# A thinner background share, a second buffer for raw columns, and a first pair turned in smaller pieces

## The chip, the cores and the metric

The kernel runs on one core of one Trainium2 chip. The metric is the device time of one execution in microseconds (us); 1149.14 us is the median of three runs of the kernel before (1148.28 to 1150.97). Beside them stands one execution that the hardware profiler recorded.

## The reference, cut to what matters

```python
def _attn_ref(q, k, v):                      # (4, 8, 576, 64) each
    q_rot, k_rot = (rotate(q), rotate(k))    # rotary embedding, two halves of 32
    scores = scale * np.matmul(q_rot, k_rot.transpose(0, 1, 3, 2))
    scores = scores - np.max(scores, axis=-1, keepdims=True)
    attn = np.exp(scores)
    attn = attn / (np.sum(attn, axis=-1, keepdims=True) + 1e-09)
    return np.matmul(attn, v)

def reference(**kwargs):
    x = attention output as (2304, 512)
    x = g1(x @ w_in) @ w_out                 # 512 -> 2048 -> 512
    return g2(x @ w_in2) @ w_out2            # 512 -> 2048 -> 512
```

g1 is a piecewise square, g2 is s times the square of the positive part, plus b. Everything is float32.

## The kernel before, in words

**Arithmetic.** Most operands of TensorE are split into a high part, rounded to the fast float32 format that TensorE takes, and the rest as a low part; a product is then made of three matmuls (high by high, high by low, low by high). ScalarE writes the high parts, VectorE or GpSimd the low parts. The weights arrive as 64-bit floats and are converted by a chain of two ScalarE, four VectorE and four GpSimd instructions for every 512 columns (`Slice.convert`, lines 115 to 134).

**Attention.** The 32 (batch, head) pairs are taken two heads at a time: 16 pairs of heads, four for each batch. Every pair is cut into 9 units, so there are 144 units. A unit is 128 rows of scores of one head against all 576 keys (unit 4 of a pair takes the last 64 rows of both heads): `qk` (line 325) runs the score matmuls (L339) into one of two PSUM tiles `sc`, VectorE takes the negated row maximum (L341), ScalarE the exponential (L346, which frees `sc`), then `tmain` transposes the result on TensorE (L361), and after units 4 and 8 of a pair `finish` multiplies by v (L387 to L394) and scales.

Before its scores a pair is turned by its rotary angles. `rope_pair` (line 273) multiplies by the table `tab_sb` (L279) and adds (L281); `lay_q` (line 287) writes each head's q as a high part in that head's own 64 partitions (ScalarE, L294) and the low part in the other 64 (VectorE, L295); `lay_k` (line 297) writes k's high part `kh` into both partition halves and its low part `kz` into one. For the first pair `lay_k` copies the high part on ScalarE (L315), has the second copy made by a DMA that SP issues (L316), and has GpSimd write the low part (L317). The first pair is turned in two pieces of 288 columns, all of it ahead of unit 0 (lines 468 to 475). Pair i+1 is turned during pair i: q at the pair's unit 0, k at unit 2 (`do_load`, line 515).

**Background work ("items").** When the four pairs of a batch are done, the first layer can begin on that batch's columns. `beside` (line 441) is a generator: it first loads raw columns `xs` from memory and splits them into `xh` and `xl` (`split_x`, line 432; four loads for each chunk of 288 columns, one `xs` buffer), lets 4 turns pass (LEAD), and then yields once after each item of 12 matmuls at line 171 (4 items `h` with their activation, then 4 items `y` with their store, for each chunk and group of weights). Three such jobs of 20, 52 and 20 turns (LEAD among them) are appended at steps 41, 75 and 111, 92 turns in all. `do_fill` (line 566) runs once in each of the steps n = 48 to 147 and hands `run_fill` a share of a turn: 0.85 below step 90 and 0.98 from there. What is left after the last step runs at once (`while fill: run_fill(1.0)`, line 579). A share left over when no job is waiting is forgotten (line 504).

**Order.** One program order is given; a scheduler that simulates the engines decides at build time in which order each engine gets its instructions (for TensorE until line 687, from where its order is as written). `issue_after(x)` puts the instructions of a block behind x, but only those on x's own engine. `first`, the last instruction that laying the first pair's k returns, is a DMA on SP; so the later loads on SP stand behind it (lines 476 and 575).

**After attention.** Five stages (lines 691 to 695) run the remaining columns of the first layer and the whole second one, matmul behind matmul.

Of the kernel before, what the change touches and what calls it, by code (L numbers as in the profile page):

```python
# [8 lines left out]
F32 = mybir.dt.float32  # L9
# [4 lines left out]
AF = mybir.ActivationFunctionType  # L14
ALU = mybir.AluOpType
AX = mybir.AxisListType
# [3 lines left out]
B, H, S, D = 4, 8, 576, 64  # L20
# [3 lines left out]
P = 128  # L24
# [35 lines left out]
N1 = 288  # L60
# [3 lines left out]
def kernel(ctx, tc, qq, kk, vv, tab, ww1, ww2, s, b, out):  # L64
    nc = tc.nc
# [14 lines left out]
    def pool_tt(out, in0, in1, op, dim=-1):  # L80

        n = out.shape[dim]
        free = 1
        for x in out.shape[1:]:
            free *= x
        k = min(n, -(-free // PW))
        for i in range(k):
            c = [slice(None)] * len(out.shape)
            c[dim] = slice(n * i // k, n * (i + 1) // k)
            c = tuple(c)  # L90
            nc.gpsimd.tensor_tensor(out=out[c], in0=in0[c], in1=in1[c], op=op)  # L91
# [3 lines left out]
    def split(dst_hi, dst_lo, src, hi_eng, lo_eng):  # L95
        if hi_eng is nc.scalar:
            made.append(nc.scalar.copy(dst_hi, src).ins)  # L97
        else:
            hi_eng.tensor_copy(dst_hi, src)
        tt = pool_tt if lo_eng is nc.gpsimd else nc.vector.tensor_tensor  # L100
        tt(out=dst_lo, in0=src, in1=dst_hi, op=ALU.subtract)  # L101
# [2 lines left out]
    HW = 512  # L104


    exps, tps = {}, {}

    class Slice:

# [113 lines left out]
    m2 = p1.enter_context(tc.tile_pool(name="m2", bufs=2, reuse_waits="tile"))  # L224
# [10 lines left out]
    tab_sb = att.tile([P, 2, S], F32, name="tab_sb")  # L235
# [4 lines left out]
    qk_in, v_in, stacks = {}, {}, {}  # L240

    WHOLE = [slice(0, S)]
    HALVES = [slice(0, 288), slice(288, S)]

    def load_qk(i, nm, pieces=WHOLE):
        bb, hp = divmod(i, NP)
        t = att2.tile([P, 2, S], F32, tag="qkin", name=f"{nm}in", bufs=QB)
        for c in pieces:
            nc.sync.dma_start(out=t[:, :, c], in_=(qq if nm == "q" else kk)[bb, hp, :, :, c])
        qk_in[nm, i] = t  # L250
# [22 lines left out]
    def rope_pair(i, nm, mul, add, lo_eng, pieces=WHOLE):  # L273

        t = qk_in.pop((nm, i))
        tt = {nc.gpsimd: pool_tt, nc.vector: nc.vector.tensor_tensor}
        last = None
        for c in pieces:
            tt[mul](out=t[:, :, c], in0=t[:, :, c], in1=tab_sb[:, :, c], op=ALU.mult)  # L279
            r = t[:, 1, c]  # L280
            tt[add](out=r, in0=t[:, 0, c], in1=r, op=ALU.add)  # L281
            last = (lay_q if nm == "q" else lay_k)(i, t, c, lo_eng)
        return last

    SELF = [slice(0, D), slice(D, P)]

    def lay_q(i, t, c, lo_eng):

        st = stacks["q", i] = qs_t[i % 2]
        r = t[:, 1, c]  # L290
        for j in range(2):
            own, other = SELF[j], SELF[1 - j]
            at = slice(j * QW + c.start, j * QW + c.stop)
            nc.scalar.activation(st[own, at], r[own], AF.Copy, scale=0.125)  # L294
            nc.vector.scalar_tensor_tensor(out=st[other, at], in0=r[own], scalar=0.125, in1=st[own, at], op0=ALU.mult, op1=ALU.subtract)  # L295

    def lay_k(i, t, c, lo_engs):
        if c.start == 0:
            stacks["k", i] = att.tile([P, 2, S], F32R, tag="kh", name="kh", bufs=2), kz_t[i % 2]
        kh, kz = stacks["k", i]  # L300
        tt = {nc.gpsimd: pool_tt, nc.vector: nc.vector.tensor_tensor}
        r = t[:, 1, c]
        if i > 0:
            hi, lo = t[:, 0, c].bitcast(F32R), r.bitcast(F32R)
            nc.scalar.copy(hi, r)
            pool_tt(out=lo, in0=r, in1=t[:, 0, c], op=ALU.subtract)
            for j in range(2):
                own = SELF[j]
                for rows in SELF:
                    nc.sync.dma_start(out=kh[rows, j, c].bitcast(F32), in_=t[own, 0, c])  # L310
                m = nc.sync.dma_start(out=kz[own, j, c].bitcast(F32), in_=t[own, 1, c])
            return m.ins
        for j in range(2):
            own, other = SELF[j], SELF[1 - j]
            nc.scalar.copy(kh[own, j, c], r[own])  # L315
            m = nc.sync.dma_start(out=kh[other, j, c].bitcast(F32), in_=kh[own, j, c].bitcast(F32))  # L316
            tt[lo_engs[j]](out=kz[own, j, c], in0=r[own], in1=kh[own, j, c], op=ALU.subtract)  # L317
        return m.ins

# [5 lines left out]
    def qk(i, k):  # L325
        if k == 0:
            sums_t[i] = att2.tile([P, 9], F32, tag="sums", name="sums")
        j, t = UNITS[k]
        sc = ps_s.tile([P, 2, 512], F32, tag="sc", name="sc")
        if j is None:  # L330
            places = [(0, 512), (1, S + D)]
        else:
            places = [(j, t * P + j * (QW + D))]
        straight = [[(0, 0, 288)], [(0, 288, 288)]]
        moved = [[(0, D, 288)], [(0, 352, 224), (224, 0, D)]]
        for half in range(2):
            todo = [(stacks["q", i][:, c:c + P], r[:, h], w) for h, c in places for r in stacks["k", i] for w in (moved if j is None and h == 0 else straight)[half]]
            for m, (l, r, (o, k0, n)) in enumerate(todo):
                nc.tensor.matmul(sc[:, half, o:o + n], l, r[:, k0:k0 + n], start=m == 0, stop=m == len(todo) - 1)  # L339
        nm = att.tile([P, 1], F32, tag="nm", name="nm", bufs=4)  # L340
        nc.vector.tensor_reduce(out=nm, in_=sc[:, :, :288], axis=AX.XY, op=ALU.max, negate=True)  # L341
        if j != 1:
            p_t[i, t] = att.tile([P, 2 * S], F32, tag="p", name="p", bufs=PB)
        p = p_t[i, t][:, S * (j == 0):S * (j == 0) + S]
        col = 4 if j is None else 2 * t + j + t // 2
        exps[i * 9 + k] = nc.scalar.activation(p, sc[:, :, :288], AF.Exp, bias=nm, scale=1.0, accum_out=sums_t[i][:, col:col + 1]).ins  # L346
        if j is None:
            nc.scalar.copy(p_t[i, t][:, S:S + D], p[:, 512:])
# [83 lines left out]
    def split_x(c):  # L432
        xh = m1.tile([P, KD, N1], F32R, tag="xh", name="xh")
        xl = m1.tile([P, KD, N1], F32R, tag="xl", name="xl")
        for k in range(KD):
            xs = m2.tile([P, N1], F32, tag="xs", name="xs", bufs=1)
            nc.sync.dma_start(out=xs, in_=xd[k, :, c * N1:(c + 1) * N1])
            split(xh[:, k, :], xl[:, k, :], xs, nc.scalar, nc.gpsimd)
        return xh, xl
# [31 lines left out]
        if c is HALVES[0]:  # L471
            load_qk(0, "k", HALVES)
    load_qk(0, "q", HALVES)
    first = rope_pair(0, "k", nc.vector, nc.vector, [nc.gpsimd, nc.gpsimd], HALVES)
    rope_pair(0, "q", nc.vector, nc.vector, None, HALVES)
    with tc.issue_after(first):
        load_qk(1, "k")
        load_qk(1, "q")
# [17 lines left out]
    def run_fill(budget):  # L496
        nonlocal done
        done += budget
        while fill and done > 0:
            try:  # L500
                done -= next(fill[0])
            except StopIteration:
                fill.pop(0)
        if not fill:
            done = 0.0
# [7 lines left out]
            qk(i, k)  # L513

    def do_load(n):
        if n < len(units):
            i, k = units[n]
            if i + 1 < NPAIR:
                if k == 0:
                    rope_pair(i + 1, "q", nc.gpsimd if i else nc.vector, nc.vector, None)  # L520
                elif k == 2:
                    rope_pair(i + 1, "k", nc.gpsimd, nc.gpsimd, [nc.gpsimd, nc.vector])
                elif k == 3:
                    load_v(i + 1)
                elif k in (4, 6) and i + 2 < NPAIR:
                    load_qk(i + 2, "q" if k == 4 else "k")

        if n in range(33, 51, 2) or n in range(70, 110, 4):
            with tc.issue_after(exps[n - 14]):
                convert()  # L530

        if n in PARK_AT and parking:
            with tc.issue_after(exps[n - 4]):
                parking.pop(0).park(wst, scratch)
# [31 lines left out]
    def do_fill(n):  # L566
        if n < 48:
            return
        with tc.issue_after(exps[min(n, len(units)) - 4]):
            run_fill(0.85 if n < 90 else 0.98)  # L570

    acts = {"q": do_qk, "l": do_load, "t": do_t, "a": do_av, "f": do_fill}
    for n in range(len(units) + LA):
# [106 lines left out]
    def cut(n0, n1, n):  # L680

        k = -(-(n1 - n0) // n)
        at = [n0 + (n1 - n0) // 16 * i // k * 16 for i in range(k + 1)]
        return [(a, b - a) for a, b in zip(at, at[1:])]
# [5 lines left out]
    a, b, c, d = cut(last, NT, N2A), cut(0, last, N2), cut(last, NT, N2), cut(0, NT, N2)  # L690
# [57 lines left out]
```

## Time and profile before

| | us |
|---|---|
| median of three runs | 1149.14 |
| the profiled execution, its own time | 1153.25 |
| the profiled execution, its span (first to last instruction) | 1151.5 |
| TensorE (PE) busy in the span | 1098.2 |
| ScalarE (ACT) busy | 696.0 |
| VectorE (DVE) busy | 603.2 |
| GpSimd (POOL) busy | 533.0 |

PE is the matmul engine; PEld is the loading of its stationary operand, which overlaps. SP is the engine that issues the DMAs. L339 is line 339 of the kernel. "Idle before" is the time that an engine stood still ahead of an instruction, and the arrow names what ended it. Matmuls are pipelined and their ends are modelled, so a busy PE is not PE at its peak. Durations below come from the one profiled execution; it took 4.1 us more than the median of the runs.

### The profile page before, as it was taken

How to read it: one execution, taken by the hardware profiler on the slowest of the kernel's cores; microseconds unless marked ns; L12 is line 12 of the kernel's file. 1: busy time of each engine (PE TensorE's matmuls, PEld its weight loads, DVE VectorE, ACT ScalarE, POOL GpSimd, SP SyncE). 2: the span in 40 equal slices, each digit the busy share in tenths (PEclk: the TensorE clock that was granted, in tenths of full speed). 3: DMA queues.
4: the chain of work that ended last, by engine and by line, in shares of the span. 5: the costliest groups of instructions: out<-in, count | busy, mean ns of one | idle time of the engine just before them, and what ended most of it. 6: DMA issues, size and time to landing. Idle time of an engine off the chain costs nothing.

```text
span 1151.5 us, 18669 instructions
## 1 busy us (share of the span) xinstructions
PE 1098.2 (95%) x6720; PEld 984.0 (85%) x6720; DVE 603.2 (52%) x999; ACT 696.0 (60%) x1466; POOL 533.0 (46%) x716
## 2 busy tenths in 40 slices
PE   4898889899989999999999999999999999999998
PEld 3566688688888988999999999999888889888887
DVE  6788878877666574455565645434333342221221
ACT  4676767766667765565554544377666666555443
POOL 6888878875544230355655634424432452111000
PEclk9999899999999999999999999999999999999999
DMA  7665645554554441544544533313322322321210
GB/s 218 170 198 141 176 143 172 181 158 123 150 170 131 145 140 45 179 144 153 150 137 147 146 121 109 88 58 102 96 80 86 115 91 68 99 66 43 67 50 34
DMA packets 90076, 140.75 MB, mean 122 GB/s; under 512 B 28928, under 2 KB 67072, under 8 KB 89984
## 3 DMA queue, kind: packets, MB, share of 16 engines
q1 hardware_dynamic: 89984, 139.56, 40.0%
q8 instruction: 53, 0.87, 0.3%
q14 instruction: 39, 0.32, 0.1%
HBM read 95.22 MB, written 30.74 MB: 109 GB/s over the span
## 4 chain that ended last, share of the span: by engine, by line
PE 75%; POOL 5%; DVE 5%; DMA 4%; ACT 3%; issue 3%; SPq 1%; POOLq 0%; ACTq 0%
PE hps L171 29%; PE yps L662 10%; PE yps L663 10%; PE yps L661 10%; PE sc L339 4%; DMA xs<-xd 3%; PE av L387 3%; PE h L171 3%; PE y L171 3%; PE tp L361 2%; POOL kin L91 2%; ACT p L346 1%; DVE nm L341 1%; POOL xl L91 1%; POOL wm L91 1%
## 5 line engine op out<-in xcount | busy, mean ns | idle before, releaser
L171 PE MATMUL hps<-xh,w 128*128 128x464 f32 (+5 forms) x1216 | 344.0, 348 | 0.0
L171 PEld LDWEIGHTS hps<-xh,w 128*128 128x128 f32 x1216 | 221.7, 188 | 14.8
L661 PE MATMUL yps<-gh,w 128*128 128x464 f32 (+5 forms) x608 | 211.7, 348 | 0.0
L662 PE MATMUL yps<-gl,w 128*128 128x464 f32 (+5 forms) x608 | 211.5, 348 | 0.1
L663 PE MATMUL yps<-gh,w 128*128 128x464 f32 (+5 forms) x608 | 211.6, 348 | 0.0
L171 PE MATMUL hps<-xl,w 128*128 128x464 f32 (+5 forms) x608 | 211.5, 348 | 0.0
L91 POOL TENSOR_TENSOR xl<-xs,xh 128x232 fp32r<-128x232 f32 (+5 forms) x172 | 125.4, 754 | 177.5 <-ACT xh L97 177.0
L101 DVE TENSOR_TENSOR gl<-ar,gh 128x464 fp32r<-128x464 f32 (+1 forms) x80 | 59.4, 743 | 264.7 <-ACT gh L97 264.7
L91 POOL TENSOR_TENSOR wm<-wm,w 128x256 f32<-128x256 f32 x112 | 98.7, 901 | 204.0 <-ACT w L132 180.8
L339 PE MATMUL sc<-kh,qs 128*128 128x288 f32 x336 | 104.3, 331 | 40.5 <-ACT p L346 26.1
L341 DVE TENSOR_REDUCE nm<-sc 128x1 f32<-128x576 f32 x144 | 107.1, 751 | 51.1 <-PE sc L339 50.1
L346 ACT ACTIVATE p<-sc,nm 128x576 f32<-128x576 f32 x144 | 106.7, 744 | 27.0 <-DVE nm L341 25.2
L662 PEld LDWEIGHTS yps<-gl,w 128*128 128x128 f32 x608 | 114.1, 188 | 7.8 <-DVE gl L101 0.3
L663 PEld LDWEIGHTS yps<-gh,w 128*128 128x128 f32 x608 | 114.1, 188 | 7.4
L661 PEld LDWEIGHTS yps<-gh,w 128*128 128x128 f32 x608 | 114.1, 188 | 7.4
L171 PEld LDWEIGHTS hps<-xl,w 128*128 128x128 f32 x608 | 114.1, 188 | 7.3
L202 ACT ACTIVATE ar<-hps 128x464 f32<-128x464 f32 (+1 forms) x80 | 44.4, 555 | 123.0 <-PE hps L171 122.4
L339 PEld LDWEIGHTS sc<-kh,qs 128*128 128x128 f32 x336 | 64.9, 196 | 60.9 <-ACT p L346 35.3
L101 DVE TENSOR_TENSOR gl<-ac,gh 128x288 fp32r<-128x288 f32 (+3 forms) x112 | 75.6, 675 | 39.2 <-ACT gh L97 38.5
L339 PE MATMUL sc<-kz,qs 128*128 128x288 f32 x336 | 95.3, 303 | 0.6 <-DMA kz<-kin 0.6
L361 PE MATMUL tp<-ident,p 128*128 128x128 f32 x576 | 90.1, 280 | 0.5 <-DVE ac L194 0.5
L91 POOL TENSOR_TENSOR w<-wm,wa 128x256 fp32r<-128x256 f32 x112 | 87.5, 798 | 1.4 <-DVE wa L131 1.4
(84 smaller groups left out, 1988.6 us busy)
## 6 DMA issues: line engine op xcount, KB each, us to landing
wraw<-in_ww SPq DMA_DIRECT2D x64, 512.0 KB, 3.9
kin<-in_k SPq DMA_DIRECT2D x15, 576.0 KB, 4.1
qin<-in_q SPq DMA_DIRECT2D x15, 576.0 KB, 4.3
kh<-kin SPq DMA_DIRECT2D x60, 144.0 KB, 2.6
xs<-y1d SPq DMA_DIRECT2D x32, 232.0 KB, 2.5
xs<-xd SPq DMA_DIRECT2D x44, 144.0 KB, 2.5
yd<-ys SPq DMA_DIRECT2D x40, 144.0 KB, 2.5
xd<-u SPq DMA_DIRECT2D x16, 288.0 KB, 2.4
```

Of the source, the lines that this page charges most:

```text
L91: nc.gpsimd.tensor_tensor(out=out[c], in0=in0[c], in1=in1[c], op=op)
L101: tt(out=dst_lo, in0=src, in1=dst_hi, op=ALU.subtract)
L171: m = nc.tensor.matmul(out_ps, l, r, start=(i == 0), stop=(i == n - 1))
L202: nc.scalar.activation(r, h, AF.Relu)
L339: nc.tensor.matmul(sc[:, half, o:o + n], l, r[:, k0:k0 + n], start=m == 0, stop=m == len(todo) - 1)
L341: nc.vector.tensor_reduce(out=nm, in_=sc[:, :, :288], axis=AX.XY, op=ALU.max, negate=True)
L346: exps[i * 9 + k] = nc.scalar.activation(p, sc[:, :, :288], AF.Exp, bias=nm, scale=1.0, accum_out=sums_t[i][:, col:col + 1]).ins
L361: m = nc.tensor.transpose(v[:, c, :], p[:, c * P:(c + 1) * P], ident)
L387: nc.tensor.matmul(ps[j * D:(j + 1) * D, :n], v[:, kt, j, :], pt[g][:, kt, j, :], start=kt == 0, stop=False)
L661: nc.tensor.matmul(acc, wh, gh, start=f == 0, stop=False)
L662: nc.tensor.matmul(acc, wh, gl, start=False, stop=False)
L663: nc.tensor.matmul(acc, wl, gh, start=False, stop=last)
```

## The change

- `run_fill` is handed 0.62 of a turn below step 76 and 0.92 from there (before: 0.85 below step 90, 0.98 from there).
- `xs`, the tile of raw columns in `split_x`, gets two buffers in place of one.
- For the first pair, the second copy of k's high part is written by ScalarE from the turned k; the DMA at L316 goes. `first` is then a ScalarE instruction, and so `issue_after(first)` holds back ScalarE's instructions, no longer SP's.
- The first pair's q is turned in three pieces (columns 0 to 127, 128 to 287, 288 to 575) in place of two. Ahead of unit 0 stand k and the first piece alone, with head 0 before head 1; the second piece follows in step 0, the third in step 1, behind the maximum of unit 0 on VectorE.
- The second pair's q is turned at unit 1 in place of unit 0, its VectorE instructions behind the maximum of unit 1; the ScalarE instructions of its k stand behind the exponential of unit 2.

```diff
-    def lay_q(i, t, c, lo_eng):
+    def lay_q(i, t, c, lo_eng, heads=range(2)):
...
-        for j in range(2):
+        for j in heads:
...
-            nc.scalar.activation(st[own, at], r[own], AF.Copy, scale=0.125)
-            nc.vector.scalar_tensor_tensor(out=st[other, at], in0=r[own], scalar=0.125, in1=st[own, at], op0=ALU.mult, op1=ALU.subtract)
+            h = nc.scalar.activation(st[own, at], r[own], AF.Copy, scale=0.125)
+            m = nc.vector.scalar_tensor_tensor(out=st[other, at], in0=r[own], scalar=0.125, in1=st[own, at], op0=ALU.mult, op1=ALU.subtract)
+        return h.ins, m.ins
...
             nc.scalar.copy(kh[own, j, c], r[own])
-            m = nc.sync.dma_start(out=kh[other, j, c].bitcast(F32), in_=kh[own, j, c].bitcast(F32))
+            m = nc.scalar.copy(kh[other, j, c], r[own])
...
-            xs = m2.tile([P, N1], F32, tag="xs", name="xs", bufs=1)
+            xs = m2.tile([P, N1], F32, tag="xs", name="xs", bufs=2)
...
-    first = rope_pair(0, "k", nc.vector, nc.vector, [nc.gpsimd, nc.gpsimd], HALVES)
-    rope_pair(0, "q", nc.vector, nc.vector, None, HALVES)
+    QP = [slice(0, P), slice(P, 288), slice(288, S)]
+    turned_by(tk, HALVES[0])
+    lay_k(0, tk, HALVES[0], [nc.gpsimd, nc.gpsimd])
+    turned_by(tk, HALVES[1])
+    lay_k(0, tk, HALVES[1], [nc.gpsimd, nc.gpsimd], [0])
+    turned_by(tq, QP[0])
+    hi, rest = lay_q(0, tq, QP[0], None, [0])
+    with tc.issue_after(hi):
+        first = lay_k(0, tk, HALVES[1], [nc.gpsimd, nc.gpsimd], [1])
+    hi, rest = lay_q(0, tq, QP[0], None, [1])
...
     def do_load(n):
+        if n < 2:
+            with tc.issue_after(maxs[0] if n else rest):
+                turned_by(tq, QP[n + 1])
+                lay_q(0, tq, QP[n + 1], None)
...
-                if k == 0:
-                    rope_pair(i + 1, "q", nc.gpsimd if i else nc.vector, nc.vector, None)
+                if k == (i == 0):
+                    with ExitStack() if i else tc.issue_after(maxs[1]):
+                        rope_pair(i + 1, "q", nc.gpsimd if i else nc.vector, nc.vector, None)
                 elif k == 2:
-                    rope_pair(i + 1, "k", nc.gpsimd, nc.gpsimd, [nc.gpsimd, nc.vector])
+                    with ExitStack() if i else tc.issue_after(exps[2]):
+                        rope_pair(i + 1, "k", nc.gpsimd, nc.gpsimd, [nc.gpsimd, nc.vector])
...
-            run_fill(0.85 if n < 90 else 0.98)
+            run_fill(0.62 if n < 76 else 0.92)
```

`turned_by` is the multiplication by the table and the addition of lines 279 and 281, on VectorE; `maxs[n]` is unit n's maximum (L341) and `exps[n]` its exponential (L346).

## Rows read from the trace of the kernel before

**Rows 1.** Busy time by stretch: us, then PE, PEld, DVE, ACT, POOL, clock, DMA, GB/s.

```profile
13.30:127.20 113.90, 101.56 (x682) 72.52 (x682) 97.47 (x152) 78.09 (x179) 92.77 (x123) 0.97 0.66 190
127.20:204.80 77.60, 69.17 (x505) 60.49 (x502) 62.93 (x103) 53.23 (x130) 61.38 (x79) 0.96 0.50 147
204.80:227.00 22.20, 18.32 (x130) 13.71 (x130) 19.23 (x32) 14.63 (x36) 19.88 (x26) 0.92 0.69 217
227.00:345.30 118.30, 110.12 (x833) 97.20 (x831) 83.27 (x142) 77.85 (x194) 69.87 (x93) 0.99 0.51 148
345.30:451.10 105.80, 102.31 (x798) 90.85 (x799) 64.89 (x123) 71.12 (x179) 31.63 (x49) 1.00 0.42 125
...
480.00:1140.00 660.00, 660.00 (x3532) 616.53 (x3532) 256.55 (x416) 381.30 (x704) 243.82 (x324) 1.00 0.32 99
```

**Rows 2.** Instructions in order of time, the first 14 us: start, us, engine, line.

```profile
6.73 5.04 SPq L316 DMA_DIRECT2D kh<-kh  x4
...
8.25 0.80 DVE L279 TENSOR_TENSOR kin<-kin,tab_sb 128x576 f32<-128x576 f32 x1 [2.01 <-DMA tab_sb<-in_tab]
9.05 0.76 DVE L279 TENSOR_TENSOR qin<-qin,tab_sb 128x576 f32<-128x576 f32 x1
9.72 0.45 DVE L281 TENSOR_TENSOR kin<-kin 128x288 f32<-128x288 f32 x1
...
10.21 0.88 ACT L315 CAST kh<-kin 64x288 fp32r<-64x288 f32 x2 [3.05 <-DVE kin L281]
...
12.81 1.91 DVE L295 SCALAR_TENSOR_TENSOR qs<-qin,qs 64x288 fp32r<-64x288 f32 x4
...
13.32 0.61 PE L339 MATMUL sc<-kh,qs 128*128 128x288 f32 x1 [13.32 <-DVE qs L295]
```

**Rows 3.** ACT's instructions of line 346 (two a unit) in those stretches.

```profile
13.30:127.20 113.90, 39.35 (x96) 0.97 0.66 190
127.20:204.80 77.60, 18.47 (x45) 0.96 0.50 147
...
227.00:345.30 118.30, 26.94 (x66) 0.99 0.51 148
345.30:451.10 105.80, 25.86 (x64) 1.00 0.42 125
```

**Rows 4.** PE's and PEld's instructions of line 171 (12 an item) in those stretches.

```profile
127.20:204.80 77.60, 31.83 (x192) 27.19 (x192) 0.96 0.50 147
...
227.00:345.30 118.30, 57.29 (x354) 49.54 (x354) 0.99 0.51 148
345.30:451.10 105.80, 51.56 (x330) 45.17 (x330) 1.00 0.42 125
```

**Rows 5.** What ACT waited for, 127 to 460 us: total us, times, longest.

```profile
ACT xh L97 <- DMA xs<-xd: 22.4, 18, 3.7
ACT p L346 <- DVE nm L341: 12.3, 13, 2.3
ACT ys L464 <- PE y L171: 9.5, 7, 2.7
ACT gh L97 <- DVE ac L194: 8.5, 10, 2.2
```

**Rows 6.** What PE waited for, 127 to 460 us: total us, times, longest.

```profile
PE sc L339 <- ACT p L346: 15.5, 14, 2.0
PE y L171 <- DVE gl L101: 3.0, 3, 1.4
PE h L171 <- ACT xh L97: 2.5, 1, 2.5
```

**Rows 7.** Instructions in order of time around 323 us.

```profile
323.37 0.43 ACT L97 CAST xh<-xs 128x288 fp32r<-128x288 f32 x1 [3.73 <-DMA xs<-xd]
...
323.85 0.40 PE L171 MATMUL h<-xh,w 128*128 128x288 f32 x1 [2.54 <-ACT xh L97]
```

**Rows 8.** The chain that ended last, one item among attention's end: start, us.

```profile
453.30 1.59 PE h L171 x12
```

More of the change, by code (lines that the diff above doesn't have):

```diff
@@ L104 @@
     HW = 512
-    exps, tps = {}, {}
+    exps, tps, maxs = {}, {}, {}
     class Slice:
@@ L285, with lay_k @@
     SELF = [slice(0, D), slice(D, P)]
-    def lay_q(i, t, c, lo_eng):
+    def lay_q(i, t, c, lo_eng, heads=range(2)):
         st = stacks["q", i] = qs_t[i % 2]
         r = t[:, 1, c]
-        for j in range(2):
+        for j in heads:
             own, other = SELF[j], SELF[1 - j]
             at = slice(j * QW + c.start, j * QW + c.stop)
-            nc.scalar.activation(st[own, at], r[own], AF.Copy, scale=0.125)
-            nc.vector.scalar_tensor_tensor(out=st[other, at], in0=r[own], scalar=0.125, in1=st[own, at], op0=ALU.mult, op1=ALU.subtract)
-    def lay_k(i, t, c, lo_engs):
-        if c.start == 0:
+            h = nc.scalar.activation(st[own, at], r[own], AF.Copy, scale=0.125)
+            m = nc.vector.scalar_tensor_tensor(out=st[other, at], in0=r[own], scalar=0.125, in1=st[own, at], op0=ALU.mult, op1=ALU.subtract)
+        return h.ins, m.ins
+    def lay_k(i, t, c, lo_engs, heads=range(2)):
+        if c.start == 0 and 0 in heads:
             stacks["k", i] = att.tile([P, 2, S], F32R, tag="kh", name="kh", bufs=2), kz_t[i % 2]
@@ L312, in lay_k @@
             return m.ins
-        for j in range(2):
+        for j in heads:
             own, other = SELF[j], SELF[1 - j]
             nc.scalar.copy(kh[own, j, c], r[own])
-            m = nc.sync.dma_start(out=kh[other, j, c].bitcast(F32), in_=kh[own, j, c].bitcast(F32))
+            m = nc.scalar.copy(kh[other, j, c], r[own])
             tt[lo_engs[j]](out=kz[own, j, c], in0=r[own], in1=kh[own, j, c], op=ALU.subtract)
@@ L340, in qk @@
         nm = att.tile([P, 1], F32, tag="nm", name="nm", bufs=4)
-        nc.vector.tensor_reduce(out=nm, in_=sc[:, :, :288], axis=AX.XY, op=ALU.max, negate=True)
+        maxs[i * 9 + k] = nc.vector.tensor_reduce(out=nm, in_=sc[:, :, :288], axis=AX.XY, op=ALU.max, negate=True).ins
         if j != 1:
@@ L473, with turned_by @@
     load_qk(0, "q", HALVES)
-    first = rope_pair(0, "k", nc.vector, nc.vector, [nc.gpsimd, nc.gpsimd], HALVES)
-    rope_pair(0, "q", nc.vector, nc.vector, None, HALVES)
+    tq, tk = qk_in.pop(("q", 0)), qk_in.pop(("k", 0))
+    def turned_by(t, c):
+        nc.vector.tensor_tensor(out=t[:, :, c], in0=t[:, :, c], in1=tab_sb[:, :, c], op=ALU.mult)
+        nc.vector.tensor_tensor(out=t[:, 1, c], in0=t[:, 0, c], in1=t[:, 1, c], op=ALU.add)
+    QP = [slice(0, P), slice(P, 288), slice(288, S)]
[8 more added lines that the diff above has]
+    hi, rest = lay_q(0, tq, QP[0], None, [1])
     with tc.issue_after(first):
```

## The prediction

> **What bounds the kernel now.** I read the busy time by stretch first, because a mean over the whole span hides that there are three regimes. From 480 us to 1140 us PE is busy for 660 of 660 us [rows 1]: there a change can gain nothing that isn't fewer matmuls, and this one removes none. Up to 13.3 us PE does nothing at all. Between lies attention, in which PE is short of busy by 12.3 us up to 127.2, by 8.4 us to 204.8, by 3.9 us to 227.0, by 8.2 us to 345.3 and by 3.5 us to 451.1 [rows 1], 36.3 us together. So whatever can be won stands in the 13.3 us of start and these 36.3 us; all the rest is PE's own work in whatever order.
>
> Next I asked what ends PE's idle time in the stretch with items: 15.5 us end with the exponential, which frees the score tile, and 2.5 us with `xh` [rows 6], so 18.0 us end at ACT. ACT is not full there (53.2 of 77.6 us, 77.9 of 118.3 us [rows 1]); it takes its instructions in order and stands in front of something that is late. The longest such thing is the load of the raw columns: 22.4 us in 18 waits [rows 5]. One of them shows the whole mechanism: ACT stands 3.73 us before `xh` until the load of `xs` lands, and PE stands 2.54 us behind it [rows 7].
>
> Last I read how an item's price depends on where it is run. Up to 127.2 us there are 48 units (96 instructions of L346, two a unit) in 113.9 us and no item: 2.37 us a unit [rows 1, 3]. From 127.2 to 204.8 us there are 22.5 units and 16 items in 77.6 us, which leaves 77.6 - 53.3 = 24.3 us, 1.52 us an item; from 227.0 to 345.3 us 33 units and 29.5 items, 118.3 - 78.2 = 40.1 us, 1.36 us an item; from 345.3 to 451.1 us 32 units and 27.5 items, 105.8 - 75.8 = 30.0 us, 1.09 us an item [rows 1, 3, 4]. Bare, an item takes 1.59 us of PE [rows 8]. So early on items are hardly hidden at all, later by a third.
>
> **The change part by part.** *Start.* PE's first matmul waits until 13.32 us for q's low part on VectorE [rows 2]. VectorE's queue is: k's second half multiplied at 8.25, when the table lands, for 0.80 us; then all of q's first half for 0.76; k's addition, 0.45, ending at 10.17; the rest of q; and only at 12.81 the first of four low parts, 0.48 each (1.91 / 4) [rows 2]. After the change only 128 of q's 288 columns stand there. k: 8.25 + 0.80 + 0.45 = 9.50. q's piece, scaled by 128/288: 0.34 + 0.20, to 10.04. On ACT two copies of k at 0.44 (0.88 / 2 [rows 2]) run from 9.5 to 10.4 if they go first, then q's high part, between 0.20 (scaled) and 0.44 (not scaled), to 10.6 to 10.8; the low part between 0.21 and 0.48, to 10.8 to 11.3. In the old order that point is 12.81 + 0.48 = 13.29. So the first scores come 2.0 to 2.5 us earlier. What is pushed back is not gone: two more pieces of q, at full price at most one old half each, go between the first maxima on VectorE, which was busy for 97.5 of 113.9 us up to unit 48 [rows 1]. At worst that gives all of it back. I take -2.0, ends -2.5 and 0. The four extra ACT copies, 4 x 0.44 = 1.8 us, are in that count or lie beside VectorE's work. The four copies by DMA that go (issued from 6.73 us on [rows 2]) ended no wait of PE's; their going lets SP issue the second pair's loads earlier, behind q's own loads in the same queue. I cost that at nothing; if these loads took a share of q's bandwidth, the start would lose part of the 2.0 us, which the end at 0 covers.
>
> *Second buffer.* The next load can be issued before the split of the last is through, so most of ACT's 18 waits go. They are 22.4 of the 52.7 us of ACT's four longest waits, 42% [rows 5]; 42% of PE's 18.0 us that end at ACT is 7.6 us. The lower end is nothing, if the exponential then waits for the maximum (12.3 us [rows 5]), the next on the list. I take -5.0, nearer to the upper end because one wait alone gave PE 2.5 us of idle time [rows 7].
>
> *Shares.* Before, job 1 (20 turns) ends at step 71; steps 72 to 74 hand out shares that are forgotten; then come 15 x 0.85 + 58 x 0.98 = 69.6 of 72 turns, and 2.4 are left over. After: 28 x 0.62 + 72 x 0.92 = 83.6 of 92 with nothing forgotten, and 8.4 left. So 6.0 items move behind the last unit at 1.59 us: +9.5. Below step 76 20.0 + 0.85 turns become 17.4, 3.5 fewer at 1.52 [rows 1, 3, 4]: -5.3. From step 76 68.7 become 66.2, 2.5 fewer at the mean of 1.36 and 1.09, 1.22: -3.1. Sum +1.1; ends 0 (every item taken out saves its bare 1.59 us) and +9.5 (nothing is saved inside). In 204.8 to 227.0 us, where PE has no item now, the 9 units took 2.47 us each, no less than elsewhere [rows 1], so filling that hole is no gain by itself. The idle PE shows there in the granted clock: 0.92, against 0.99 and 1.00 in the two stretches after it [rows 1]. Fewer items for each unit below step 76 could bring more such stretches. The Trainium skill ("TensorE: Matmul & The Clock Gate", Part 1) says that "the default state is throttled, and activity releases the throttle"; the trace agrees as far as the 0.92 goes, and by that rule this part of the sum would carry the lower clock too, which is a rival below.
>
> *Left-over items.* With 8.4 items at the end, four `y` stand right behind four `h`, with no units between them to cover the activation. A `y` that waits for its low part stood at most 1.4 us [rows 6]: +0.5, ends 0 and +1.4.
>
> **The sum:** -2.0 - 5.0 + 1.1 + 0.5 = -5.4 us. The profiled execution took 1153.25 us, 4.1 more than the median, so it would take 1147.9 us and the median falls from 1149.14 to **1143.7 us**.
>
> **The rivals.** *Slower: items inside are free.* If VectorE, GpSimd and ACT pace attention between steps 48 and 147, taking items away there shortens nothing, and six come at full price at the end. Then PE's idle time is worth less as well, and I halve the second buffer's gain to 2.5. With f for the part of 1.59 us that an item taken out gives back, the sum is -2.0 - 2.5 + 0.5 + 9.5 (1 - f): slower than the 0.2% line below f = 0.34, and +5.5, 1154.6 us, at f = 0. For it speaks that VectorE (62.9) and POOL (61.4 of 77.6 us) are nearly as busy as PE [rows 1], against it the 1.52 us an item [rows 1, 3, 4]. Chance 0.14.
>
> *Nothing gained.* Half of the start is given back to VectorE's queue and ACT waits for the maximum instead of the load: -1.0 + 0 + 1.1 + 0.5 = +0.6, 1149.7 us. Here too belongs that the shares do not do what they say, since a scheduler picks the order and may draw items forward anyway. Chance 0.18.
>
> *All of ACT's waiting goes.* PE's 18.0 us that end at ACT shrink to a third because the exponentials come on time everywhere: -12 - 2.5 + 1.6, 1136 us. Chance 0.12.
>
> *The clock.* If steps 48 to 76 ran at the 0.92 of the hole rather than at 0.96, about 95 us x 0.04 = 3.8 us come on top: 1147.5 us. The clock gate rule of the Trainium skill, named above, is the reason to list it. Chance 0.06, because in the 227.0 to 345.3 us stretch with items the clock was 0.99 [rows 1].
>
> **The numbers.** The forecast has the other 0.50, with its own range 1139 to 1146.8 us (ends -10.1 for -2.5 - 7.6, and the 0.2% line). The range of 8 in 10 leaves out the far half of the gain rival and the far half of the slower one: 1137 to 1152 us. A measurement of this kernel can tell about 0.2%, 2.3 us: faster means under 1146.8, slower over 1151.4. Faster: 0.50 and 0.12, a third of the clock's 0.06, and 0.03 of the "nothing" case: 0.67. Slower: 0.14. Same: the other 0.19.
>
> **What would show it.** The first matmul at 10.8 to 11.3 us; unit 48 about 2 us earlier; ACT's waits for `xs` from 22 us to a few, and PE's idle time behind the exponential down by about 5 us between 127 and 460; items without a hole between steps 71 and 76; the last unit earlier by some 15 us, with about 6 more items behind it. The forecast is wrong if the last unit comes earlier by less than the 9.5 us that the moved items cost, if the wait for the load is replaced by one for the maximum of the same length, or if unit 48 is not earlier.

## The result, and the profile after

The changed kernel takes **1139.22 us** (median of six runs, 1137.34 to 1140.45); the kernel before, on the same chip, took 1150.06 us (six runs, 1148.1 to 1153.25). The ratio is 0.9897, 95% interval 0.9882 to 0.9913: 10.8 us faster where 5.4 were forecast. The profiled execution of after took 1140.24 us, its span 1138.4; that of before took 1153.25 and 1151.5 us.

First the busy time by stretch, cut at the same events as [rows 1]: the first matmul, the exponential of unit 48, that of unit 112 and that of the last unit. The columns are those of [rows 1].

```profile
11.50:124.60 113.10, 100.16 (x682) 71.67 (x682) 97.64 (x158) 79.95 (x186) 94.46 (x121) 1.00 0.64 180
124.60:334.90 210.30, 194.67 (x1469) 169.46 (x1468) 167.12 (x277) 146.39 (x358) 157.17 (x204) 0.98 0.55 164
334.90:430.20 95.30, 92.99 (x732) 83.25 (x732) 61.10 (x117) 67.58 (x174) 27.55 (x43) 1.00 0.41 125
430.20:461.40 31.20, 31.20 (x245) 29.19 (x241) 11.02 (x26) 16.45 (x45) 6.88 (x9) 1.00 0.32 91
461.40:1138.40 677.00, 672.67 (x3602) 627.73 (x3601) 259.00 (x420) 382.09 (x705) 244.04 (x324) 1.00 0.32 100
```

Beside it the same view for PE's and PEld's instructions of line 171 alone, 12 an item, as in [rows 4].

```profile
124.60:334.90 210.30, 82.44 (x527) 72.21 (x528) 0.98 0.55 164
334.90:430.20 95.30, 44.66 (x291) 39.36 (x289) 1.00 0.41 125
430.20:461.40 31.20, 26.02 (x192) 25.62 (x192) 1.00 0.32 91
```

Read against [rows 1, 4], the span's 13.1 us come from these places. The start is 1.8 us shorter (13.3 to 11.5). Up to unit 48 it is 113.1 us instead of 113.9. From there to unit 112 it is 210.3 us instead of 77.6 + 22.2 + 118.3 = 218.1, with 44 items (527 / 12) instead of 45.5. From unit 112 to the last it is 95.3 us instead of 105.8, with 24 items instead of 27.5. Everything behind takes 31.2 + 677.0 = 708.2 us instead of 1151.5 - 451.1 = 700.4, because five more items stand there (12 have run after the last exponential, 7 before the change). -1.8 - 0.8 - 7.8 - 10.5 + 7.8 = -13.1.

The second way to cut the same 13.1 us is by PE's own account. For the same 6720 matmuls it was busy for 1098.2 us and is now busy for 1091.7 (-6.5); it was idle for 53.3 us of the span and is now idle for 46.7 (-6.6). Of the idle time 1.8 us went at the start. Between the first matmul and the last unit PE was short of busy by 36.3 us and is now short by 113.10 - 100.16 + 210.30 - 194.67 + 95.30 - 92.99 = 30.9 us: -5.4. Behind the last unit 0.6 us came in addition.

How much of the 6.5 us of busy time is PE's clock can't be read from the clock column, because that column counts the time ahead of the profile's first clock record as full. The record, a rise from 1.2 to 2.4 GHz, stands at 21.7 us before and at 28.1 us after, and the matmuls agree: a score matmul of 288 columns takes 0.44 us ahead of it and 0.29 to 0.30 behind. One row before, one after (the columns are those of [rows 2]):

```profile
22.27 0.29 PE L339 MATMUL sc<-kz,qs 128*128 128x288 f32 x1
```

```profile
26.52 0.44 PE L340 MATMUL sc<-kz,qs 128*128 128x288 f32 x1
```

From the first matmul to the rise PE ran at 1.2 GHz for 8.4 us before and for 16.5 after; from there to the last unit the records show 1.2 GHz for 20.5 us before and for 10.2 after. Together that is 28.9 and 26.7 us. So the clock gave back far less than the column's 0.97 and 1.00 suggest, and what it did give back is not all the change's doing, as the last section shows.

What ACT and PE waited for between 124 and 460 us (columns as in [rows 5, 6]):

```profile
ACT p L347 <- DVE nm L342: 19.3, 19, 2.8
ACT xh L97 <- DMA xs<-xd: 8.0, 8, 3.9
...
PE sc L340 <- ACT p L347: 11.9, 11, 3.0
```

The wait for the raw columns went from 22.4 to 8.0 us. The wait for the maximum rose from 12.3 to 19.3, by half of those 14.4 us. PE's idle time behind the exponential fell by 3.6 us, from 15.5 to 11.9.

What the second buffer did can be seen without any sum, in ACT's splits of one chunk near 305 us. Before the change (columns as in [rows 2]; the third of the four splits, at 323.37, stands in [rows 7]):

```profile
304.66 0.43 ACT L97 CAST xh<-xs 128x288 fp32r<-128x288 f32 x1 [0.44 <-PE h L171]
...
315.59 0.43 ACT L97 CAST xh<-xs 128x288 fp32r<-128x288 f32 x1 [0.61 <-DMA xs<-xd]
...
326.95 0.43 ACT L97 CAST xh<-xs 128x288 fp32r<-128x288 f32 x1 [0.36 <-DMA xs<-xd]
```

After it:

```profile
306.52 0.77 ACT L97 CAST xh<-xs 128x288 fp32r<-128x288 f32 x2
...
311.18 0.42 ACT L97 CAST xh<-xs 128x288 fp32r<-128x288 f32 x1
311.79 0.45 ACT L97 CAST xh<-xs 128x288 fp32r<-128x288 f32 x1
```

From the first split to the start of the last it was 22.3 us and is 5.3. Before, three of the four splits stand behind their own load; after, none does.

Last the start, in order of time:

```profile
7.32 1.31 DVE L478 TENSOR_TENSOR kin<-kin,tab_sb 128x576 f32<-128x576 f32 x1 [0.64 <-DMA tab_sb<-in_tab]
8.17 1.10 POOL L91 TENSOR_TENSOR kz<-kin,kh 64x288 fp32r<-64x288 f32 x1
8.54 1.01 DVE L478 TENSOR_TENSOR qin<-qin,tab_sb 128x256 f32<-128x256 f32 x1
...
10.86 0.31 ACT L294 ACTIVATE qs<-qin 64x128 fp32r<-64x128 f32 x1
11.21 0.29 DVE L295 SCALAR_TENSOR_TENSOR qs<-qin,qs 64x128 fp32r<-64x128 f32 x1 [1.09 <-ACT qs L294]
...
11.55 0.61 PE L340 MATMUL sc<-kh,qs 128*128 128x288 f32 x1 [11.55 <-DVE qs L295]
...
12.74 0.99 DVE L478 TENSOR_TENSOR qin<-qin,tab_sb 128x320 f32<-128x320 f32 x1
13.77 0.80 DVE L479 TENSOR_TENSOR qin<-qin 128x160 f32<-128x160 f32 x1
14.48 0.75 DVE L342 TENSOR_REDUCE nm<-sc 128x1 f32<-128x576 f32 x1
15.31 0.74 ACT L347 ACTIVATE p<-sc,nm 128x576 f32<-128x576 f32 x1
...
20.80 0.74 ACT L347 ACTIVATE p<-sc,nm 128x576 f32<-128x576 f32 x1 [1.20 <-DVE nm L342]
```

The first matmul starts 1.77 us earlier than in [rows 2], but the first maximum stands on VectorE behind the second piece of q and starts at 14.48 us, where before it was 14.68; the first exponential starts at 15.31 instead of 15.48. Of 1.8 us, 0.2 are left one step further on. At unit 1 the lead has turned round: its exponential starts at 20.80 us, where before it was 16.44, and that of unit 8 at 35.95 instead of 32.63.

### The profile page after: what moved, and what is told of

The parts are those of the page before. It is cut to its first block, busy times and chain, and to the rows that moved or that the text cites. A ratio compares the mean times of both kernels' runs of the same rounds, so it can differ in the third digit from the quotient of the medians.

```text
span 1138.4 us, 18638 instructions
## 1 busy us (share of the span) xinstructions
PE 1091.7 (96%) x6720; PEld 981.3 (86%) x6720; DVE 600.3 (53%) x1003; ACT 696.9 (61%) x1472; POOL 536.2 (47%) x716
## 4 chain that ended last, share of the span: by engine, by line
PE 78%; DVE 7%; DMA 4%; ACT 4%; POOL 4%; issue 2%; SPq 1%; POOLq 0%; ACTq 0%; DVEq 0%
PE hps L171 30%; PE yps L682 10%; PE yps L684 10%; PE yps L683 10%; PE sc L340 5%; PE h L171 3%; PE av L388 3%; PE tp L362 3%; PE y L171 2%; POOL kin L91 2%; DVE nm L342 2%; ACT p L347 2%; DMA kin<-in_k 1%; DVE qs L295 1%; DVE wm L129 1%
## 5 line engine op out<-in xcount | busy, mean ns | idle before, releaser
L340 PE MATMUL sc<-kh,qs 128*128 128x288 f32 x336 | 103.7, 330 | 32.6 <-ACT p L347 20.6
L347 ACT ACTIVATE p<-sc,nm 128x576 f32<-128x576 f32 x144 | 106.7, 743 | 32.6 <-DVE nm L342 32.0
L101 DVE TENSOR_TENSOR gl<-ac,gh 128x288 fp32r<-128x288 f32 (+3 forms) x112 | 72.6, 650 | 40.6 <-ACT gh L97 40.0
```

## The experiments

Each kernel was timed beside the kernel before, whose median was 1151.43 to 1152.72 us there; the ratios are to that, with 95% intervals.

### One part alone

**The shares alone** (one buffer, old start):

```diff
-            run_fill(0.85 if n < 90 else 0.98)
+            run_fill(0.62 if n < 76 else 0.92)
```

> The kernel before with the new shares alone (0.62 below step 76, 0.92 from there). Theory of the forecast: six items move behind the last unit, +1.1 us and +0.5 us for their activations, so 1150 to 1152 us, with ACT still waiting some 20 us for the raw columns. Rival (thin shares even the work out and close the hole of steps 71 to 76): -5 us or more, 1145 us or less, with PE's idle time behind the exponential down without any change of the buffer.

1144.65 us, ratio 0.9942 (0.9919 to 0.9965). ACT's wait for the raw columns stayed; its row, and PE's idle time behind the exponential:

```profile
ACT xh L97 <- DMA xs<-xd: 25.9, 21, 3.3
...
PE sc L339 <- ACT p L346: 12.9, 12, 2.5
```

So this kernel is 0.58% faster, where I had summed the shares to a loss of 1.1 us. Whether the shares themselves gain that is not shown: below, 0.01 of a share moves the time by as much.

**The second buffer alone:**

```diff
-            xs = m2.tile([P, N1], F32, tag="xs", name="xs", bufs=1)
+            xs = m2.tile([P, N1], F32, tag="xs", name="xs", bufs=2)
```

> The kernel before with two buffers for raw columns alone. Theory of the forecast: -5 us, 1145 us, ACT's waits for the raw columns from 22 us to under 8, PE's idle time behind the exponential down by about 5 us between 127 and 460 us. Rival (another wait takes the place of the load's): 1149 to 1151 us, with ACT's wait for the maximum longer by about what the load's wait loses.

1137.66 us, ratio 0.9875 (0.9852 to 0.9897): this one word gives 14 us, and gives no less than the whole change.

```profile
ACT p L346 <- DVE nm L341: 14.9, 17, 2.7
...
ACT xh L97 <- DMA xs<-xd: 9.7, 13, 1.9
...
PE sc L339 <- ACT p L346: 8.5, 9, 2.9
```

Here PE's idle time behind the exponential fell by 7.0 us (15.5 to 8.5), near the upper end of 7.6 that I had given the term, and the wait for the maximum rose by 2.6 us only. The page's chain of work that ended last tells the same. Before:

```profile
PE hps L171 29%; PE yps L662 10%; PE yps L663 10%; PE yps L661 10%; PE sc L339 4%; DMA xs<-xd 3%; PE av L387 3%; PE h L171 3%; PE y L171 3%; PE tp L361 2%; POOL kin L91 2%; ACT p L346 1%; DVE nm L341 1%; POOL xl L91 1%; POOL wm L91 1%
```

With the second buffer alone:

```profile
PE hps L171 30%; PE yps L661 10%; PE yps L663 10%; PE yps L662 10%; PE y L171 5%; PE sc L339 5%; PE h L171 4%; PE av L387 4%; PE tp L361 3%; POOL kin L91 2%; DVE nm L341 1%; POOL qin L91 1%; ACT p L346 1%; DMA qin<-in_q 1%; DMA kz<-kin 1%
```

The load of `xs` was 3% of the chain and is no longer on the list. I had not taken this number into the prediction. It points at the load, but it is no price: 3% of 1151.5 us is some 35 us of chain, two and a half times the 14 us that the buffer gave at most. In the other kernels the load has 2 to 3% with one buffer (the shares alone, the start alone, and two more below) and none to 1% with two or three.

**The start alone**, all the rest of the diff; against the changed kernel:

```diff
-            xs = m2.tile([P, N1], F32, tag="xs", name="xs", bufs=2)
+            xs = m2.tile([P, N1], F32, tag="xs", name="xs", bufs=1)
-            run_fill(0.62 if n < 76 else 0.92)
+            run_fill(0.85 if n < 90 else 0.98)
```

> The kernel before with the new start alone (second copy of k by ScalarE, q in three pieces, second pair's turning later). Theory of the forecast: -2.0 us, 1148 us. Rival (the pieces pushed between the first maxima give it all back): the first exponential no earlier than 15.2 us, unit 8 later, and 1150 us. Second rival: unit 48 earlier by 2.6 us for another reason, the order of the next pairs, and 1147 us.

1153.52 us, ratio 1.001 (0.9994 to 1.0026): no gain. The rival's signs are there, the first exponential at 15.18 us and that of unit 8 at 35.31 instead of 32.63; yet unit 48 starts at 124.61 us instead of 127.23, which the last section takes up.

### Two parts, and the whole with one buffer

Shares and buffer, with the old start; against the kernel before:

```diff
-            xs = m2.tile([P, N1], F32, tag="xs", name="xs", bufs=1)
+            xs = m2.tile([P, N1], F32, tag="xs", name="xs", bufs=2)
-            run_fill(0.85 if n < 90 else 0.98)
+            run_fill(0.62 if n < 76 else 0.92)
```

> The kernel before with new shares and two buffers, the old start. Theory of the forecast: the parts add, 1149.9 + 1.6 - 5 = 1146 to 1147 us. Rival (the two need each other, since with one buffer ACT stands at the load whatever the share): 1141 us or less, which is more than the two runs alone add up to.

1143.14 us, 0.9917 (0.9896 to 0.9937).

Buffer and start; against the changed kernel:

```diff
-            run_fill(0.62 if n < 76 else 0.92)
+            run_fill(0.85 if n < 90 else 0.98)
```

> Two buffers and the new start, the old shares. If the start is worth nothing (as alone), 1137 to 1139 us, the same as two buffers alone. If it is worth the 2 us or so that the whole change has over shares with two buffers, 1135 us. If the start and the buffers get into each other's way, over 1140 us.

1139.05 us, 0.9889 (0.9868 to 0.991).

Shares and start, with one buffer; against the changed kernel:

```diff
-            xs = m2.tile([P, N1], F32, tag="xs", name="xs", bufs=2)
+            xs = m2.tile([P, N1], F32, tag="xs", name="xs", bufs=1)
```

> The whole change with one buffer for raw columns. Theory (the buffer is what pays): ACT's waits for the raw columns back at 22 to 26 us, and 1145 us, as the shares alone. Rival (shares and buffer pay for the same idle time, so that either will do): 1140 to 1142 us, near the whole change.

1146.4 us, 0.9946 (0.9928 to 0.9965).

With these every part can be read in several surroundings. The buffer: from before -1.25%, on the start alone -1.21% (1.001 to 0.9889), on the shares alone -0.25% (0.9942 to 0.9917), on both -0.49% (0.9946 to 0.9897). The start: +0.1% from before, +0.14% on the buffer, +0.04% on the shares, -0.2% on both; none of the four is beyond its interval. The shares: -0.58% from before and -0.64% on the start, but +0.42% on the buffer and +0.08% on buffer and start. The parts don't add: the product of the three alone is 0.9942 x 0.9875 x 1.001 = 0.983, the whole change has 0.9897. It would fit this that buffer and shares mend in part the same thing, but that is not shown: the 0.01 of a share below moves the time by as much as the parts differ.

ACT's wait for the load goes by the buffer alone: it is 20.5 to 25.9 us between 124 and 460 us in the five profiles with one buffer, and 7.4 to 11.6 us in the nine with two or three. Shares and start with one buffer:

```profile
ACT xh L97 <- DMA xs<-xd: 23.3, 17, 3.5
```

Buffer and start:

```profile
ACT xh L97 <- DMA xs<-xd: 9.6, 12, 2.1
```

### A third buffer

Against the kernel before:

```diff
-            xs = m2.tile([P, N1], F32, tag="xs", name="xs", bufs=1)
+            xs = m2.tile([P, N1], F32, tag="xs", name="xs", bufs=3)
```

> Three buffers for raw columns and nothing else. Theory (the load's latency was the whole of it): ACT's remaining waits of 9.7 us for the raw columns shrink further and the time falls by 1 to 3 us below that of two buffers, 1135 to 1137 us. Rival (two buffers already cover the load; what is left are waits for the columns to be written): 1137 to 1139 us, with the same waits.

1139.98 us, 0.9892 (0.9873 to 0.9911), not beyond the interval of two buffers.

```profile
ACT xh L97 <- DMA xs<-xd: 7.4, 7, 2.0
...
PE sc L339 <- ACT p L346: 6.4, 7, 2.4
```

Both waits are 2 us shorter than with two, and the time is no better. No gain of a third buffer is shown.

### The two halves of the shares, on two buffers

The lower share below step 76 alone:

```diff
-            run_fill(0.85 if n < 90 else 0.98)
+            run_fill(0.62 if n < 76 else 0.85 if n < 90 else 0.98)
```

> Two buffers and the thin share below step 76 alone (0.62, then 0.85 and 0.98 as before). Theory (with two buffers, an item taken out of the early steps gives back less than its 1.59 us): some 3 to 4 us slower than two buffers alone, 1141 us. Rival (the thin early share is good and the 0.92 later does the harm): 1136 us or less.

1148.11 us, 0.9958 (0.9943 to 0.9974): 0.84% slower than the buffer alone. Fewer items below step 76 mean more behind the last unit, and there PE once stood for an item's `y` that ScalarE copied late out of PSUM (its waits between 440 and 475 us):

```profile
PE yps L661 <- ACT ys L464: 2.2, 1, 2.2
```

The later shares alone:

```diff
-            run_fill(0.85 if n < 90 else 0.98)
+            run_fill(0.85 if n < 76 else 0.92)
```

> Two buffers and the new share from step 76 alone (0.85 below 76, 0.92 from there). Theory (the harm is done in the early steps): within 1.5 us of two buffers alone, 1137 to 1139 us. Rival (harm done late): 1141 us or more.

1143.65 us, 0.993 (0.9906 to 0.9954): 0.56% slower than the buffer alone. So each half is slower by itself (+0.84% and +0.56%), and both together are slower by 0.42%. No price per item gives that, and none of the three is larger than what the next section finds for 0.01 of a share.

### How much a hair's breadth of share moves

To learn what such differences are worth I changed the share by 0.01, which hands out at most 42 x 0.01 = 0.4 of a turn less in the 42 steps from 48 to 89.

```diff
-            run_fill(0.85 if n < 90 else 0.98)
+            run_fill(0.84 if n < 90 else 0.98)
```

On the kernel before:

> The kernel before with 0.84 in place of 0.85, a change that moves a fifth of an item. Theory (with one buffer the time hangs on where the scheduler happens to put the loads): a difference of several us in either direction, 1144 to 1155 us. Rival (the time follows the amount of work moved): within 1.5 us of the kernel before.

1156.46 us, 1.0033 (1.002 to 1.0046).

On two buffers:

> Two buffers with 0.84 in place of 0.85. Theory (the order that falls out of the scheduler is worth some us with two buffers as well, and 0.85 was a lucky one): 1139 to 1143 us. Rival (the time follows the amount of work moved): 1137 to 1138.5 us.

1146.99 us, 0.995 (0.9933 to 0.9968): 0.76% slower than 0.85 on two buffers, some 8.6 us for an amount of work that at 1.59 us an item [rows 8] is worth 0.7 us at most. The stretches 125 to 209.3 and 209.3 to 303 us show where. With 0.85:

```profile
125.00:209.30 84.30, 76.69 (x573) 66.05 (x573) 72.63 (x120) 61.84 (x149) 69.03 (x89) 0.98 0.57 164
209.30:303.00 93.70, 88.78 (x668) 77.66 (x665) 70.13 (x119) 63.76 (x158) 62.67 (x82) 0.96 0.50 148
```

With 0.84:

```profile
125.00:209.30 84.30, 75.42 (x538) 64.99 (x539) 69.57 (x112) 57.94 (x141) 65.94 (x83) 0.94 0.54 151
209.30:303.00 93.70, 85.03 (x620) 73.59 (x618) 66.17 (x115) 60.21 (x147) 54.06 (x74) 0.95 0.53 153
```

In the same 178 us PE gets through 83 fewer matmuls (573 + 668 against 538 + 620); it is short of busy for 5 us more and its clock is lower. The shares go to a scheduler that picks the order of everything else; that another order with other stalls makes the difference is likely, but it is argued and not shown. Which instruction's place makes these 8.6 us was not found, and stays open. The two probes give a fifth pair for the buffer: 1.0033 to 0.995, -0.83%. The mean of the five pairs is -0.81%, 9.3 us; all five have the buffer faster, from -0.25% to -1.25%, and by their scatter the mean is known to about 0.5% either way (an estimate from these five).

### Holding the second and third piece of q back

If the start is worth nothing because q's second piece stands ahead of the first maximum, then forcing that piece behind it should bring the 1.8 us through. On buffer and start:

```diff
-            with tc.issue_after(maxs[0] if n else rest):
+            with tc.issue_after(maxs[n]):
```

> Two buffers, old shares, the new start, and the second piece of q put behind the maximum of unit 0 (the third behind that of unit 1). Theory (the pieces stand in front of the first maximum on VectorE and eat the earlier matmul): first exponential at about 13.7 us in place of 15.2, and 1 to 1.5 us below the run without this order, 1137.5 us. Rival (the first 120 us are paced by other work, whatever the start): the exponential earlier, unit 48 not, 1139 us.

1147.17 us, 0.9952 (0.9937 to 0.9968): 0.64% slower than without the edit. Instructions of the first units, in order of time:

```profile
13.39 0.76 DVE L342 TENSOR_REDUCE nm<-sc 128x1 f32<-128x576 f32 x1 [0.17 <-PE sc L340]
14.18 0.74 ACT L347 ACTIVATE p<-sc,nm 128x576 f32<-128x576 f32 x1 [1.29 <-DVE nm L342]
17.51 0.61 PE L340 MATMUL sc<-kh,qs 128*128 128x288 f32 x1 [1.33 <-DVE qs L295]
20.34 1.95 DVE L279 TENSOR_TENSOR qin<-qin,tab_sb 128x1152 f32<-128x1152 f32 x1
26.64 2.98 DVE L295 SCALAR_TENSOR_TENSOR qs<-qin,qs 64x288 fp32r<-64x288 f32 x4
28.21 0.58 PE L340 MATMUL sc<-kh,qs 128*128 128x288 f32 x1 [3.21 <-DVE qs L295]
```

The first maximum and exponential do come 1.0 us earlier (the exponential at 14.18 instead of 15.22 without the edit). Then the bill arrives: at 17.51 PE stands 1.33 us and at 28.21 it stands 3.21 us for pieces of q that VectorE has not made, the second time behind the next pair's q of 1152 columns at 20.34. Unit 4's exponential starts at 32.6 us, with the pieces in their old place at 27.7 and in the kernel before at 24.8. Unit 48 is at 130.8 instead of 124.5. So at neither of the two places that were tried is q's work hidden: VectorE is busy for 13.4 of the 16.2 us from 13.4 to 29.6 us here, and for 14.7 with the pieces in their old place. PE's clock adds to it: it rose to 2.4 GHz at 32.2 us here, at 28.0 without the edit and at 21.7 in the kernel before. Of the 0.64%, 7.3 us, that this kernel loses, 5.0 are there at unit 4 and 6.3 at unit 48. To put the next pair's q behind the first pair's third piece was not tried.

## Why the prediction was right, and where not

**What bounds the kernel: right.** All that was won stands in the start and in attention; behind it five items were added and cost 7.8 us, 1.56 each, as [rows 8] has them.

**The second buffer: right mechanism, size too small in the mean.** "I take -5.0", ends -7.6 and 0. It measured -14 us alone, -9.3 us in the mean over five surroundings, and -5.6 us as the last part added to the whole change; the scatter of the five leaves room for 3 to 15 us, and only two of the pairs, from before and on the start alone, lie clear of its range. The step that gave too little there is the scaling: "42% of PE's 18.0 us that end at ACT is 7.6 us". That holds only the idle time directly behind ACT. With the buffer alone 7.0 us of it did go, but PE's whole idle time fell by more: from the first matmul to the last unit PE was short of busy by 437.8 - 401.5 = 36.3 us before and, from 13.3 to 430.0 us (the last unit is at 435.2), by 416.7 - 390.3 = 26.4 us with the buffer, and for the same matmuls it was busy for 5.6 us less in the span. Which stalls the other 3 us of idle time were was not followed up. The fear at the lower end, that the wait moves to the maximum, came true in part and most in the whole change (12.3 to 19.3 us).

**The start: wrong.** "I take -2.0", ends -2.5 and 0: it came out at the end at 0. The four pairs have a mean of +0.02%, each known to some 0.2 to 0.3%, so the times alone can't well tell 0 from 2 us (0.17%); the traces show what became of them. The first matmul came at 11.55 us, 0.25 later than the latest forecast, and that with luck: the table landed at 7.32 us, 0.9 earlier than in the profile of before (it is 7.62 to 8.40 us in the other profiles with the old start and 7.71 to 8.88 in those with the new one). From the landing to the first matmul it was 4.2 us, where 2.6 to 3.1 were forecast. The step that failed is what came after the first matmul, where I let the two other pieces of q go "between the first maxima" and took none of their price into the -2.0. The second piece stands ahead of the first maximum, and at both places that were tried the pieces come due by unit 4. PE's clock belongs to this step as well, and I had no term for it: it rose at 21.7 us before and at 28.1 after (20.6 to 27.9 in the nine profiles with the old start, 26.0 to 32.2 in the five with the new one). By unit 48 the lead is back in part: the four profiles of the new start without the held-back pieces have it at 123.4 to 124.7 us, those of the old start at 124.2 to 127.3.

The scaled price failed too: q's 128 columns were to take 0.34 us for the multiplication and took 1.01, with POOL's `kz` write running from 8.17 to 9.27 us beside it, where the 576 elements of 288 columns took 0.76 [rows 2]. In the four other profiles of the new start no POOL instruction runs beside it, and it takes 0.41 or 0.42 us, as in that of buffer and start:

```profile
9.05 0.41 DVE L478 TENSOR_TENSOR qin<-qin,tab_sb 128x256 f32<-128x256 f32 x1
```

The Trainium skill ("GPSIMD Engine Reference", section Specifications) says that GpSimd's interfaces to SBUF are shared with VectorE, with contention for VectorE instructions that have two inputs in SBUF; these rows agree, with 1.01 us beside POOL against 0.41 without.

**The shares: the sum was near, its working is not borne out.** +1.1 was forecast; by surroundings the runs give -0.6% to +0.4%, and +0.1 to +0.4% (1 to 5 us) with the buffer, for which the sum was made. But 0.01 of a share moved the time by 3.8 us in one kernel and 8.6 in the other, so a sum of items by prices per item can't be told right or wrong here: what it left out, the order that the scheduler falls into, is as large as every term in it. One slip of its own: 0.85 of the "3.5 fewer" below step 76 is a turn of LEAD, which holds no item, so it should have been 2.6 items at 1.52 and 3.4 at 1.22, 8.1 us in place of 8.4, and +1.4. The hole without items in 204.8 to 227.0 us is filled in after (every 10 us from 140 to 220 hold matmuls of items) and no gain of its own is seen from it.

**The left-over items: right in size, at another place.** +0.5 was forecast for a `y` that waits for its low part. Among the left-over items there is no such wait: PE is busy for 31.20 of 31.20 us behind the last unit, with five more items there, not six. But the stage right behind them stands 0.5 us for an item's `y` that ScalarE copies out of PSUM, a wait that the kernel before does not have (waits behind the last unit, columns as in [rows 6]):

```profile
PE yps L682 <- ACT ys L465: 0.5, 1, 0.5
```

**The rivals.** That items inside are free, and so the change is slower, fell: attention is 21 us shorter to the last unit (450.4 to 429.4 us) against 7.8 us behind it. Nothing gained fell. That all of ACT's waiting goes was nearest in time (1136 us) but not in mechanism: 8.0 us of the wait for the load and 19.3 for the maximum remain. The clock did not fall from steps 48 to 76: it is 0.96 from 124.6 to 206.0 us, the exponentials of units 48 and 75, as it was from 127.2 to 204.8 us before [rows 1].

**The signs.** Borne out: ACT's waits for `xs` (22.4 to 8.0 us), no hole, the last unit earlier by more than 15 us. In size less than said: PE's idle time behind the exponential (-3.6, said -5). Not a sign of anything, as it turned out: unit 48 came 2.6 us earlier, as forecast, but for the larger part from another cause, told below.

**Total.** By the runs' own pairs: buffer -5.6 us (shares and start to the whole), shares and start -6 us (before to shares and start), of which the start is nothing; -11.9 by the ratio, -10.8 by the medians. In the other order the buffer has -14 and the rest gives 2.5 back. The forecast of -5.4 had the sign and the main part right; half of the 10.8 us it did not have. In the first order the missing part lies in the shares, -0.58% (6.7 us) for +1.1, in the other in the buffer, and either way it is about as large as what 0.01 of a share moves. So which term it belongs to stays open, and that the sum came as near as it did is in part luck: the times show nothing of the start's 2 us, and the rest gave some 7 us more than forecast.

A version that is at least as good as both is the one-word edit alone: 1137.66 us, 0.9875 (0.9852 to 0.9897), which overlaps the whole change's interval; that it is faster than the whole change is not shown.

## What to carry to other kernels

A staging tile with one buffer, filled by a load and emptied by an engine that takes its instructions in order, turns a chunk's loads into a chain. Two numbers of the trace bracket its price: the idle time that the bounding engine shows behind it (7.6 us here at most) was too low for the mean of the pairs, 9.3 us, and its share of the chain of work that ended last (some 35 us here) far too high. Before an early start is counted as a gain, follow the work that was pushed back to the first unit that needs it, on the engine that makes it. Where a scheduler picks the order, measure first what a meaningless change of its inputs does (here 0.33 and 0.76%), and believe a part's effect only when it shows in several surroundings.

## What the runs showed of the hardware that was not expected

**The granted clock in the same order.** Up to about 70 us the kernel before, the one with two buffers and the one with the later shares alone issue the same instructions in the same order on every engine. Yet in the profiled execution of before the granted clock fell to 1.2 GHz at 35.4 us, in that of the later shares at 34.6, and with two buffers not before 164.6. Ahead of that PE stood for the second pair's k, which SP copies by DMA. Before:

```profile
33.05 0.37 PE L339 MATMUL sc<-kh,qs 128*128 128x288 f32 x1 [0.95 <-DMA kh<-kin]
```

Later shares:

```profile
33.49 0.37 PE L339 MATMUL sc<-kh,qs 128*128 128x288 f32 x1 [1.39 <-DMA kh<-kin]
```

With two buffers PE does not stand at that matmul. At the next copy (`kz`) it stands in all three, for 0.64, 0.41 and 0.79 us. So the same order ran with a DMA that landed about 1 us sooner or later, and the clock fell behind the late ones; three profiles don't show more than that. PE's rows for 32 to 55 us, before:

```profile
32.00:55.00 23.00, 20.20 (x134) 13.98 (x132) 16.80 (x25) 12.81 (x30) 19.43 (x28) 0.93 0.60 174
```

Two buffers:

```profile
32.00:55.00 23.00, 21.12 (x150) 14.37 (x149) 18.21 (x30) 15.97 (x38) 21.14 (x29) 1.00 0.63 183
```

Later shares: 134 matmuls as well, clock 0.93.

That is 134 matmuls against 150 in the same 23 us. Unit 18's exponential starts at 58.1 us in the two with the drop and at 55.6 in the one without, 2.5 us for nothing in the code. That is the larger part of the 2.6 us by which unit 48 came earlier in the profile of after (127.23 to 124.65 us): without the new start it is at 125.3 us with the shares alone, at 125.9 with the buffer alone and at 125.1 with both, and at 127.3 with the later shares, which have the fall too. So the profiles of two kernels are compared only after their clocks are, and a stage's gain is taken from the runs.

**VectorE beside POOL.** On two inputs, 128x256 took 1.01 us and 128x320 0.99 us in the rows of the start above, both with POOL at work, where 128x576 takes 0.76 [rows 2]. By price per element that is off by a factor of two to three. It is not so beside every POOL instruction: at 15.15 us in the same profile q's 128x576 took 0.74 us with POOL at work all the while.
